# Low parts of transposed queries and keys, taken ahead of the evacuation copy of a step

## The chip, the core and the metric

One core of a Trainium2 chip runs the kernel. Its engines work side by side, each through its own queue of instructions in order: TensorE (PE; weight loads are PEld), VectorE (DVE), ScalarE (ACT), GpSimd (POOL), and SyncE (SP), which here only issues transfers. The metric is the device time of one execution in microseconds, less being better; the median of several executions is compared.

## What is computed

Attention in which the 12 heads are mixed twice, by `w_pre` ahead of the softmax and by `w_post` behind it, and then a two-layer network with a squared ReLU:

```python
# batch 4, heads 12, sequence 448, head size 64; d_ff 2048
scores = 1 / np.sqrt(64) * np.matmul(q, k.transpose(0, 1, 3, 2))
scores = np.einsum('bhij,hg->bgij', scores, w_pre)
scores = scores - np.max(scores, axis=-1, keepdims=True)
attn = np.exp(scores)
attn = attn / (np.sum(attn, axis=-1, keepdims=True) + 1e-09)
attn = np.einsum('bhij,hg->bgij', attn, w_post)
x = np.matmul(attn, v).transpose(0, 2, 1, 3).reshape(4 * 448, 12 * 64)
r = np.maximum(x @ w_in, 0.0)
out = (s * (r * r) + b) @ w_out
```

## The kernel before

Products that need full precision are made of three matmuls each: a number is split into a high part, which ScalarE writes as a rounded copy, and a low part, the difference, which VectorE takes. High times low, low times high and high times high are summed in one PSUM bank.

The attention part is cut into 16 chunks (4 per batch, 110 or 118 queries each), and a chunk into blocks of up to 10 queries, 180 blocks in all. A block has 120 rows: 10 queries by 12 heads. The loop at the end of the function runs one step `s` for each block, and several blocks are under way in each step: block `s + 5` is brought from the score tile `S` by a transfer (`relayout`, tile `blk`), block `s + 2` is split on GpSimd (`split`, tile `hl`), block `s` goes through `premix` (three matmuls into `pm`, L603; VectorE's maximum, L605; ScalarE's exponential with its sum, L610, and the sum's copy, L614), block `s - 1` is normalized (VectorE's reciprocal, L622; ScalarE's high part `eh`, L624; VectorE's `remainder`, L631), block `s - 3` goes through `postmix` (twelve matmuls into `po`, L646), and block `s - 4` is evacuated from PSUM to the tile `A` (`evacuate`, VectorE's copy at L662). There are two `po` banks, taken in turn.

Besides, a table (`plan`) says in which step the work of the chunks around falls. `prep_k` and `prep_q` transpose keys and queries on TensorE (`trk`, L457; `trq`, L479) into a PSUM tile with the tag `sc`; ScalarE writes the high part (`Tk`, L463; `Tq`, L483), and the low part is put on a list, `later`. A query tile is prepared in two halves, of four head pairs (here called full-sized) and of two (half-sized). `qk_pair` computes the scores of a head pair (six matmuls, `sc`, L504), in the same PSUM tile `sc`, which has one buffer, and ScalarE copies them to `S` (L514). So `sc` goes round: transpose, high and low part, score matmuls, copy to `S`, next transpose. `av_pair` (`xp`, L532, with ScalarE's copy `xs`, L554) multiplies with the values.

`low_parts` takes what stands on `later`, one VectorE subtraction each, all of them at L239. The loop calls it at the two places that the change's diff shows, and `prep_k`, `prep_q` and `qk_pair` call it at their start. The order on each engine is the order in which the code is written: no scheduler moves anything. VectorE also converts weights of the network, one operation per step where there is room (L157 to L181). Behind the loop come the two layers, at L254 and L311.

Of the kernel before, what the change touches and what calls it, by code (L numbers as in the profile page):

```python
# [21 lines left out]
def talking_heads_attention__then__act_relu2_kernel(  # L22
# [163 lines left out]
    def place_w(n):  # L186
        w_pool[n].tile([P, 2, 3 * P], F32R, tag=f"w{n}", name=f"place_{n}", bufs=1)

    def convert_step(upto):

        if done["run"] is None:
            if done["conv"] >= min(upto, len(units)):
                return False
            done["run"] = conversion(done["conv"])
        try:
            next(done["run"])
        except StopIteration:
            done["run"] = None
            done["conv"] += 1
        return True  # L200
# [13 lines left out]
    def load_x(r, b, kc):  # L214
        raw = rp.tile([P, S], F32, tag="xraw", name=f"xraw_{r}_{b}_{kc}", bufs=NKC)
        nc.sync.dma_start(raw, xd[b][kc])
        xraw_t[r, b, kc] = raw

    def split_x(r, b, kc):
        raw = xraw_t.pop((r, b, kc))  # L220
        if b == 1:

            if kc % 2 == 0:
                x_u["g"] = mp.tile(
                    [P, 2, PT], F32R, tag=f"g{kc // 2}_1", name=f"xg_{r}_{kc}", bufs=1
                )
            x = x_u["g"][:, :, kc % 2 * S:kc % 2 * S + S]
        else:
            x = rp.tile([P, 2, S], F32R, tag="x", name=f"x_{r}_{b}_{kc}", bufs=NKC)
        nc.scalar.activation(x[:, 0, :], raw, AF.Copy)  # L230
        later.append((x[:, 1, :], raw, x[:, 0, :]))
        x_u[r, b, kc] = x
# [3 lines left out]
    def low_parts():  # L236
        while later:
            o, x, hi = later.pop(0)
            nc.vector.tensor_tensor(out=o, in0=x, in1=hi.bitcast(F32), op=ALU.subtract)  # L239
# [323 lines left out]
    def qk_pair(ci, p):  # L563
        low_parts()
        for m in range(3):
            qk_part(ci, p, m)
# [9 lines left out]
    def relayout(t):  # L576
        ci, i0, ni = blocks[t]
        blk = blkp.tile([BP, S], F32, tag="blk", name=f"blk_{t}", bufs=LD)
        nb = first[ci + 1] - first[ci]
        r = t - first[ci]  # L580
        nc.sync.dma_start(blk[:ni * H, :], s_t[ci][r:r + nb * (ni - 1) + 1:nb, :, :])
        blk_t[t] = blk

    def split(t):
        n = blocks[t][2] * H
        blk = blk_t.pop(t)
        hl = blkp.tile([BP, 2, S], F32R, tag="hl", name=f"hl_{t}", bufs=2)
        nc.gpsimd.tensor_scalar(hl[:n, 0, :], blk[:n], 1.0, 0.0, op0=ALU.mult, op1=ALU.add)  # L588
        nc.gpsimd.tensor_tensor(  # L589
            out=hl[:n, 1, :], in0=blk[:n], in1=hl[:n, 0, :].bitcast(F32), op=ALU.subtract  # L590
        )
        hl_t[t] = hl

    def premix(t):
        n = blocks[t][2] * H
        hl = hl_t.pop(t)

        tag = "px" if t % 3 == 2 else "pm"
        pm = ps.tile([P, 512], F32, tag=tag, name=f"pm_{t}", bufs=banks.count(tag))
        for _ in range(2 if t < first[1] - 1 else 1 if t < first[1] + 3 else 0):  # L600
            nc.tensor.matmul(pm, keep[:, :P], keep, start=True, stop=True)
        for m, (w, x) in enumerate(((wpre_lo, 0), (wpre_hi, 1), (wpre_hi, 0))):
            nc.tensor.matmul(pm[:n, :S], w[:n, :n], hl[:n, x, :], start=(m == 0), stop=(m == 2))  # L603
        st = smp.tile([BP, 4], F32, tag="st", name=f"st_{t}")
        nc.vector.tensor_reduce(  # L605
            out=st[:n, 0:1], in_=pm[:n, :S], axis=AX.X, op=ALU.max, negate=True
        )

        e = pm[:, :S]
        nc.scalar.activation(e[:n], e[:n], AF.Exp, bias=st[:n, 0:1], accum_out=pm[:n, S:S + 1])  # L610
        e_t[t] = (e, st)

        total = pm[:, S:S + 1]
        nc.scalar.activation(  # L614
            st[:n, 2:3], total[:n], AF.Copy, scale=2.0 ** -15, bias=1e-9 * 2.0 ** -15
        )

    def normalize(t):

        n = blocks[t][2] * H  # L620
        e, st = e_t[t]
        nc.vector.reciprocal(st[:n, 3:4], st[:n, 2:3])  # L622
        eh = blkp.tile([BP, 2, S], F16, tag="eh", name=f"eh_{t}", bufs=3)
        nc.scalar.activation(eh[:n, 0, :], e[:n], AF.Copy, scale=st[:n, 3:4])  # L624
        eh_t[t] = eh

    def remainder(t):
        n = blocks[t][2] * H
        e, st = e_t.pop(t)
        eh = eh_t[t]  # L630
        nc.vector.scalar_tensor_tensor(  # L631
            out=eh[:n, 1, :], in0=e[:n], scalar=st[:n, 3:4], in1=eh[:n, 0, :],
            op0=ALU.mult, op1=ALU.subtract,
        )

    def postmix(t):
        ci, i0, ni = blocks[t]
        n = ni * H
        eh = eh_t.pop(t)
        if i0 == 0:  # L640
            a_t[ci] = ap_.tile([P, NC, H, CH], F32, tag="A", name=f"A_{ci}")
        po = ps.tile([P, 512], F32, tag="po", name=f"po_{t}", bufs=2)
        for c in range(NC):
            j0 = min(c * P, S - P)
            for m, (x, y) in enumerate(((1, 0), (0, 1), (0, 0))):
                nc.tensor.matmul(  # L646
                    po[:, c * BP:(c + 1) * BP],
                    eh[:n, x, j0:j0 + P],
                    wpost[:n, y].rearrange("p g i -> p (g i)"),
                    start=(m == 0),  # L650
                    stop=(m == 2),
                )
        po_t[t] = po

    def evacuate(t):
        ci, i0, ni = blocks[t]
        dst = a_t[ci][:, :, :, i0:i0 + ni]
        src = po_t.pop(t)[:, :NC * BP].rearrange("p (c g i) -> p c g i", c=NC, g=H)[:, :, :, :ni]
        if ci == NCH - 1:
            nc.scalar.activation(dst, src, AF.Copy)  # L660
        else:
            nc.vector.tensor_copy(dst, src)  # L662
# [6 lines left out]
    XA = 3  # L669
# [99 lines left out]
    def run_plan(step, early):  # L769

        k0 = state["next"]
        while k0 < len(plan) and plan[k0][0] < step + 1:
            _, order, _, f, args = plan[k0]
            if (order == 0) == early:
                f(*args)
            k0 += 1
        if not early:
            state["next"] = k0
            copy_x()
# [60 lines left out]
    tail = first[NCH - 1]  # L840
    for s in range(NB + 4):
        if s == tail - LD:
            early.close()
            rp = ctx.enter_context(tc.tile_pool(name="rp", bufs=1, side="right", reuse_waits="tile"))
            rp.tile([P, S], F32, tag="xraw", name="place_xraw", bufs=NKC)
            for n in range(NU_EARLY, NU_EARLY + NU_TAIL):
                w_pool[n] = rp
                place_w(n)
            rp.tile([P, X_GAP // 4], F32, tag="gap", name="gap_x", bufs=1)
            rp.tile([P, 2, S], F32R, tag="x", name="place_x", bufs=NKC)  # L850
            rp.tile([P, END_GAP // 4], F32, tag="end", name="gap_end", bufs=1)
        if s + LD < NB:
            relayout(s + LD)
        if s + LS < NB:
            split(s + LS)
        if 0 <= s - 1 < NB:
            ops = 7 * NU_EARLY
            if not later and turn["ops"] < ops * (s - CONV0) / (tail - LD - 2 * NP - CONV0):
                turn["ops"] += convert_step(NU_EARLY)
            normalize(s - 1)  # L860
        if 0 <= s - 4 < NB:
            evacuate(s - 4)
        if s <= tail - XA:
            low_parts()
        if s < NB:
            premix(s)
        low_parts()
        if s < 2:
            (build_scale, build_post)[s](*loaded_consts)
            qk_pair(1, NP - 2 + s)  # L870
        if 0 <= s - 1 < NB:
            remainder(s - 1)
        run_plan(s, True)
        if 0 <= s - 3 < NB:
            postmix(s - 3)
        run_plan(s, False)
        if 0 <= s - (tail - LD) < NKC // 2:
            for kc in range(2):
                load_x(0, 0, 2 * (s - (tail - LD)) + kc)
        if 0 <= s - (tail - XA) < NKC:  # L880
            split_x(0, 0, s - (tail - XA))
        if 0 <= s - tail < NKC:
            load_x(0, 1, s - tail)
# [111 lines left out]
```

## Time and profile before

| what | time |
|---|---|
| median of 3 runs | 938.13 us (937.76 to 938.72) |
| the profiled execution | 941.96 us |
| its span, from the first to the last instruction | 940.3 us |
| attention loop and what leads to it | to about 480 us of the span |
| the two layers | from there to the end |

The profile tells of one execution. Busy time of an engine is the sum of its instructions' times, in which an instruction that starts before its predecessor has quite ended counts in full. A wait is an engine's idle time ahead of an instruction, put down to what ended it. The chain that ended last is followed back from the last instruction, at each step to what released it or to its predecessor on its engine.

### The profile page before, as it was taken

The numbers are of one execution on the slowest core, as the hardware profiler recorded it, in microseconds if no ns is written. First come the engines' busy times: TensorE is split into PE (matmuls) and PEld (weight loads), VectorE is DVE, ScalarE is ACT, GpSimd is POOL, SyncE is SP. The second block draws the span as 40 slices with busy tenths as digits, with TensorE's granted clock in tenths as the row PEclk, the third lists the DMA queues.
The fourth block names the chain that finished last, engine by engine and source line by source line (L and its number), as shares of the span: only waits on it lengthen the run. The fifth ranks groups of instructions, "written<-read, shape, count | busy, mean of one in ns | idle before, by whom it ended". The sixth has DMA issues, their size and how long they took to land.

```text
span 940.3 us, 19909 instructions
## 1 busy us (share of the span) xinstructions
PE 917.5 (98%) x7538; PEld 786.3 (84%) x7538; DVE 655.2 (70%) x1364; ACT 567.3 (60%) x1264; POOL 396.5 (42%) x451
## 2 busy tenths in 40 slices
PE   8889999999999999999999999999999999999998
PEld 4567777777777777777789999999999999999998
DVE  3788888888888888888689139966405934976211
ACT  4687788887888888888877877221117687700000
POOL 3766677666767667767523324000002333300000
PEclk9999999999999999999999999999999999999999
DMA  4665645655466545646324213353510420255321
GB/s 99 168 166 134 165 113 148 160 149 156 123 157 158 144 122 144 164 134 184 101 73 143 76 59 85 89 172 126 177 43 26 143 93 17 75 161 185 127 93 51
DMA packets 126555, 115.22 MB, mean 123 GB/s; under 512 B 63960, under 2 KB 122348, under 8 KB 126460
## 3 DMA queue, kind: packets, MB, share of 16 engines
q1 hardware_dynamic: 116934, 102.28, 38.9%
q10 hardware_dynamic: 9366, 11.59, 3.4%
q8 instruction: 59, 0.97, 0.4%
q14 instruction: 36, 0.29, 0.1%
q0 software_dynamic: 160, 0.09, 0.1%
HBM read 58.87 MB, written 16.52 MB: 80 GB/s over the span
## 4 chain that ended last, share of the span: by engine, by line
PE 63%; ACT 17%; DVE 10%; DMA 7%; POOL 1%; issue 1%; SPq 1%; ACTq 0%; POOLq 0%; DVEq 0%
PE po L311 25%; PE ph L254 23%; ACT pm L610 6%; DMA blk<-S 5%; ACT S L514 4%; PE pm L603 4%; DVE A L662 3%; ACT eh L624 3%; PE sc L504 3%; PE xp L532 3%; PE po L646 3%; DVE st L605 2%; ACT st L614 2%; ACT xs L554 1%; PE ph_head L254 1%
## 5 line engine op out<-in xcount | busy, mean ns | idle before, releaser
L311 PE MATMUL po<-w,g 128*128 128x384 f32 x1344 | 233.5, 336 | 0.0
L311 PEld LDWEIGHTS po<-w,g 128*128 128x128 f32 x1344 | 233.0, 188 | 0.3 <-ACT ob L318 0.3
L589 POOL TENSOR_TENSOR hl<-blk,hl 120x448 fp32r<-120x448 f32 x180 | 205.9, 1144 | 15.0
L272 POOL TENSOR_TENSOR g<-h,g 128x448 fp32r<-128x448 f32 x64 | 79.4, 1240 | 280.1 <-ACT g L271 259.6
L254 PE MATMUL ph<-x,w 128*128 128x448 f32 x810 | 164.1, 362 | 0.0
L254 PEld LDWEIGHTS ph<-x,w 128*128 128x128 f32 x810 | 151.9, 188 | 10.2
L588 POOL TENSOR_SCALAR hl<-blk 120x448 fp32r<-120x448 f32 x180 | 104.6, 581 | 125.4 <-PE pm L603 102.9
L646 PEld LDWEIGHTS <-eh 120*128 120x128 f16 (+1 forms) x2160 | 115.3, 98 | 40.9 <-issue 40.5
L646 PE MATMUL po<-wpost,eh 120*128 120x120 f16 (+1 forms) x2160 | 144.7, 217 | 1.4 <-ACT A L660 1.4
L610 ACT ACTIVATE pm<-pm,st 120x448 f32<-120x448 f32 x180 | 110.1, 611 | 56.2 <-DVE st L605 55.7
L631 DVE SCALAR_TENSOR_TENSOR eh<-pm,st,eh 120x448 f16<-120x448 f32 x180 | 122.4, 680 | 26.2 <-ACT eh L624 22.9
L624 ACT ACTIVATE eh<-pm,st 120x448 f16<-120x448 f32 x180 | 114.6, 637 | 15.9 <-DVE st L622 15.6
L605 DVE TENSOR_REDUCE st<-pm 120x1 f32<-120x448 f32 x180 | 110.7, 615 | 7.4 <-PE pm L603 7.3
L662 DVE COPY A<-po 128x480 f32<-128x480 f32 x168 | 107.0, 637 | 0.1
L603 PE MATMUL pm<-hl,wpre_hi 120*120 120x448 f32 x360 | 101.9, 364 | 0.8 <-POOL hl L589 0.8
L532 PE MATMUL xp<-A,v 128*64 128x110 f32 (+1 forms) x1536 | 93.5, 265 | 0.0
L504 PE MATMUL sc<-Tk,Tq 64*110 64x448 f32 (+1 forms) x576 | 83.3, 395 | 8.4 <-DVE Tq L239 4.8
L514 ACT ACTIVATE S<-sc 110x896 f32<-110x896 f32 (+1 forms) x91 | 83.2, 914 | 10.0 <-PE sc L504 7.1
L603 PE MATMUL pm<-hl,wpre_lo 120*120 120x448 f32 x180 | 82.8, 460 | 0.1
L532 PEld LDWEIGHTS xp<-A,v 128*64 128x64 f32 x1536 | 74.2, 136 | 9.6 <-issue 0.9
L318 ACT ACTIVATE ob<-po 128x384 f32<-128x384 f32 x28 | 13.8, 493 | 98.0 <-PE po L311 86.0
L603 PEld LDWEIGHTS pm<-hl,wpre_hi 120*120 120x120 f32 x360 | 65.5, 182 | 5.6 <-POOL hl L589 1.0
(78 smaller groups left out, 981.9 us busy)
## 6 DMA issues: line engine op xcount, KB each, us to landing
blk<-S SPq DMA_DIRECT2D x172, 210.0 KB
raw<-in_moe_w_in_dram SPq DMA_DIRECT2D x32, 384.0 KB
raw<-in_moe_w_out_dram SPq DMA_DIRECT2D x32, 384.0 KB
xraw<-xd SPq DMA_DIRECT2D x48, 224.0 KB
part<-ob ACTq DMA_DIRECT2D x28, 192.0 KB
acc<-part SPq DMA_DIRECT2D x28, 192.0 KB
out_dram<-acc ACTq DMA_DIRECT2D x28, 192.0 KB
v<-in_v_dram SPq DMA_DIRECT2D x24, 192.0 KB
```

The source lines that it names most:

```text
L254: nc.tensor.matmul(ph[:, :S], w[:, i, c0:c0 + P], x[:, y, :], start=(kc == 0 and m == 0), stop=(kc == NKC - 1 and m == 2),)
L311: nc.tensor.matmul(po[:, :NO], g[:, x, c0:c0 + P], w[:, y, :], start=(f == 0 and m == 0), stop=(f == NF - 1 and m == 2),)
L514: nc.scalar.activation(s_t[ci][:n, 2 * p:2 * p + 2, :], x_t["two"][:n, :, :S], AF.Copy, scale=SCALE)
L532: nc.tensor.matmul(xp[e * D:(e + 1) * D, p % 4, :n], vt[:, e, c, :], a[:, c, 2 * p + e, :n], start=(c == 0), stop=(c == NC - 1),)
L589: nc.gpsimd.tensor_tensor(out=hl[:n, 1, :], in0=blk[:n], in1=hl[:n, 0, :].bitcast(F32), op=ALU.subtract)
L603: nc.tensor.matmul(pm[:n, :S], w[:n, :n], hl[:n, x, :], start=(m == 0), stop=(m == 2))
L605: nc.vector.tensor_reduce(out=st[:n, 0:1], in_=pm[:n, :S], axis=AX.X, op=ALU.max, negate=True)
L610: nc.scalar.activation(e[:n], e[:n], AF.Exp, bias=st[:n, 0:1], accum_out=pm[:n, S:S + 1])
L624: nc.scalar.activation(eh[:n, 0, :], e[:n], AF.Copy, scale=st[:n, 3:4])
L631: nc.vector.scalar_tensor_tensor(out=eh[:n, 1, :], in0=e[:n], scalar=st[:n, 3:4], in1=eh[:n, 0, :], op0=ALU.mult, op1=ALU.subtract,)
L646: nc.tensor.matmul(po[:, c * BP:(c + 1) * BP], eh[:n, x, j0:j0 + P], wpost[:n, y].rearrange("p g i -> p (g i)"), start=(m == 0), stop=(m = ...
L662: nc.vector.tensor_copy(dst, src)
```

## The change

Two calls in the loop change places. `low_parts()` was called behind `evacuate(s - 4)` and is now called ahead of it:

```diff
             normalize(s - 1)
+        if s <= tail - XA:
+            low_parts()
         if 0 <= s - 4 < NB:
             evacuate(s - 4)
-        if s <= tail - XA:
-            low_parts()
         if s < NB:
             premix(s)
```

`tail - XA` is three steps ahead of the last chunk's first block. The instructions of TensorE, ScalarE, GpSimd and SyncE keep their order; VectorE's differs at 46 places, 18 with a low part of keys (`Tk`) and 28 with one of queries (`Tq`), 14 of these full-sized and 14 half-sized. All 46 look alike.

VectorE at the step in which the sixth key pair of the second batch gets its low part (`Tk_5`; the last number of a name is the build's), before and after; the lines with - and + show where the subtraction stood and stands:

```order
 L631 SCALAR_TENSOR_TENSOR eh_1911<-pm_1864,st_1868,eh_1911 120x448
 L622 RECIPROCAL st_1918<-st_1918 120x1
+L239 TENSOR_TENSOR Tk_5_1942<-trk_5_1937,Tk_5_1942 128x448
 L662 COPY A_1923<-po_1924 128x48x10
-L239 TENSOR_TENSOR Tk_5_1942<-trk_5_1937,Tk_5_1942 128x448
 L605 TENSOR_REDUCE st_1958<-pm_1954 120x1
 L631 SCALAR_TENSOR_TENSOR eh_1950<-pm_1914,st_1918,eh_1950 120x448
```

The subtraction now stands directly behind the reciprocal, and the evacuation copy between it and the maximum of the step.

ScalarE at the same step, the same before and after; `Tk_5` at L463 is the high part that this subtraction reads:

```order
L610 ACTIVATE pm_1914<-pm_1914,st_1918 120x448
L614 ACTIVATE st_1918<-pm_1914 120x1
L463 ACTIVATE Tk_5_1942<-trk_5_1937 128x448
L624 ACTIVATE eh_1950<-pm_1914,st_1918 120x448
L610 ACTIVATE pm_1954<-pm_1954,st_1958 120x448
L614 ACTIVATE st_1958<-pm_1954 120x1
L514 ACTIVATE S_1617<-sc_4_1986 110x896
```

Nothing moved here: the high part follows the sum's copy (L614) that the reciprocal of this step reads, and the next exponential (L610) reads the maximum.

VectorE at a step with a half-sized low part of queries (`Tq`, two head pairs of 110 queries):

```order
 L622 RECIPROCAL st_2258<-st_2258 108x1
+L239 TENSOR_TENSOR Tq_2026<-trq_1_2276,Tq_2026 128x2x110
 L662 COPY A_1923<-po_2263 128x48x10
-L239 TENSOR_TENSOR Tq_2026<-trq_1_2276,Tq_2026 128x2x110
 L605 TENSOR_REDUCE st_2294<-pm_2290 120x1
```

The same two instructions have changed places.

## Rows read from the trace of the kernel before

**Rows 1.** The page, part 1: busy us (share of the span) and instructions.

```profile
PE 917.5 (98%) x7538; PEld 786.3 (84%) x7538; DVE 655.2 (70%) x1364; ACT 567.3 (60%) x1264; POOL 396.5 (42%) x451
```

**Rows 2.** Busy time in one stretch: us, engines (instructions), granted clock, transfers.

```profile
60.00:435.00 375.00, 366.23 (x4189) 276.97 (x4189) 325.34 (x698) 305.75 (x770) 258.79 (x303) 1.00 0.54 143
```

**Rows 3.** Waits from 60 to 435 us: us in total, times, longest.

```profile
ACT pm L610 <- DVE st L605: 48.5, 72, 1.1
...
PE sc L504 <- DVE Tq L239: 4.1, 14, 0.4
...
PE trq L479 <- ACT S L514: 2.1, 5, 1.1
...
PE sc L504 <- DVE Tk L239: 1.2, 3, 0.7
```

**Rows 4.** The chain that ended last, 222 to 234 us: start, us, what.

```profile
222.44 0.53 DVE Tk L239
222.97 0.54 DVE st L605
...
223.54 0.68 ACT pm L610 x2
...
224.41 0.81 ACT S L514
...
232.51 0.54 DVE Tk L239
...
233.09 0.86 PE sc L504 x6
```

**Rows 5.** Timeline at a full-sized low part: start, us, engine, line, operation [idle before].

```profile
119.18 0.54 ACT L463 ACTIVATE Tk<-trk 128x448 fp32r<-128x448 f32 x1
...
119.40 0.64 DVE L662 COPY A<-po 128x480 f32<-128x480 f32 x1
...
119.95 0.61 DVE L239 TENSOR_TENSOR Tk<-trk,Tk 128x448 fp32r<-128x448 f32 x1
120.48 0.61 DVE L605 TENSOR_REDUCE st<-pm 120x1 f32<-120x448 f32 x1
...
120.62 0.86 PE L504 MATMUL sc<-Tk,Tq 64*110 64x448 f32 x6
...
121.13 0.61 ACT L610 ACTIVATE pm<-pm,st 120x448 f32<-120x448 f32 x1 [0.89 <-DVE st L605]
...
122.12 0.81 PE L646 MATMUL po<-wpost,eh 120*128 120x120 f16 x12
```

**Rows 6.** Timeline of the prologue: a high part and the low part that waits for it.

```profile
16.47 0.55 ACT L463 ACTIVATE Tk<-trk 128x448 fp32r<-128x448 f32 x1 [0.46 <-PE trk L457]
...
17.05 0.62 DVE L239 TENSOR_TENSOR Tk<-trk,Tk 128x448 fp32r<-128x448 f32 x1 [0.53 <-ACT Tk L463]
```

**Rows 7.** Timeline at a half-sized low part.

```profile
138.63 0.35 ACT L483 ACTIVATE Tq<-trq 128x220 fp32r<-128x220 f32 x1
...
138.85 0.64 DVE L662 COPY A<-po 128x480 f32<-128x480 f32 x1
...
139.40 0.38 DVE L239 TENSOR_TENSOR Tq<-trq,Tq 128x220 fp32r<-128x220 f32 x1
...
139.84 0.87 PE L504 MATMUL sc<-Tk,Tq 64*110 64x448 f32 x6 [0.28 <-DVE Tq L239]
```

**Rows 8.** Timeline: copies to S and the transposes behind them, first and last place.

```profile
77.80 0.91 ACT L514 ACTIVATE S<-sc 118x896 f32<-118x896 f32 x1
...
78.83 0.37 PE L479 MATMUL trq<-ident,nq 118*128 118x118 f32 x2
...
346.07 0.91 ACT L514 ACTIVATE S<-sc 110x896 f32<-110x896 f32 x1
...
347.04 0.60 PE L479 MATMUL trq<-ident,nq 110*128 110x110 f32 x4
```

**Rows 9.** Timeline of ScalarE: a copy to S that waits for a transfer.

```profile
101.22 0.92 ACT L514 ACTIVATE S<-sc 110x896 f32<-110x896 f32 x1 [0.41 <-DMA nk<-in_k_dram]
```

## The prediction

> **What bounds the kernel now.** I read the busy times first, then the stretch of the attention loop alone, then who waited for whom there, then the chain that ended last, and at the end single places of the timeline. Over the span TensorE is busy 98% of the time and VectorE 70% [rows 1]. The change reaches only the attention loop, where 46 low parts (18 of keys, 28 of queries) change places with an evacuation copy. In 375 us of that loop TensorE is busy 366.23 us at a granted clock of 1.00, VectorE 325.34 and ScalarE 305.75 [rows 2]. So TensorE seems to be the bound, with 8.8 us of shown idle time. The waits say where some of that is: TensorE's score matmuls `sc` wait for the low part 4.1 us (queries) and 1.2 us (keys), and transposes of queries wait 2.1 us for ScalarE's copy of a score tile, `S` [rows 3]. But the longest wait is ScalarE's: the exponential at L610 waits 48.5 us, 72 times, for VectorE's maximum at L605 [rows 3].
>
> Whether that wait costs anything, the chain tells. It runs through low part (L239), maximum (L605), exponential (L610), and the copy of scores (L514) on ScalarE [rows 4]; ahead of the low part stand, in the same chain, the sum's copy, the reciprocal and the evacuation copy. This is a ring of in-order queues: ScalarE can't go on to the next exponential before the maximum is there, and the maximum stands on VectorE behind copy and low part. Of the 46 low parts the chain passes 24 in this way; 13 times it goes from the low part to the score matmuls instead, as at 232.51 [rows 4]; 9 it doesn't touch. So in the loop two bounds lie side by side: TensorE with almost no gaps, and a VectorE-ScalarE ring that is as long.
>
> **The change part by part.** No instruction is added or taken away, and only VectorE's queue is in another order. At each of 46 places the row recip, copy, low part, maximum becomes recip, low part, copy, maximum.
>
> *The new wait, full-sized low parts (32 of the 46).* The low part needs the rounded high part that ScalarE writes just before. At the place shown that copy runs from 119.18 for 0.54, to 119.72, while VectorE starts the evacuation at 119.40 and the low part at 119.95 [rows 5]. Today the evacuation covers the whole of ScalarE's copy. Moved ahead, the low part finds VectorE free at 119.40 and its input not there. In the prologue, where VectorE does wait for the same operation, it starts at 17.05 behind a copy that runs from 16.47 for 0.55, thus 0.03 us behind its end [rows 6]. So the low part would start at 119.75: 0.20 us earlier than now, with VectorE idle for 0.35 us. The evacuation follows 0.53 us later (119.95 to 120.48 is what a low part holds the queue [rows 5]), at 120.28 instead of 119.40, and the maximum 0.55 us behind that, at 120.83 instead of 120.48: **0.35 us later**. Queued behind the waiting low part are the evacuation, the maximum and the remainder; ScalarE's exponential waits for the maximum (0.89 us of idle time ended by it at 121.13 [rows 5]) and so goes 0.35 us later too.
>
> *Half-sized low parts of queries (14).* ScalarE's copy is shorter: 138.63 for 0.35, with the evacuation at 138.85 and the low part at 139.40 [rows 7]. By the same working the low part starts at 139.01, 0.39 us earlier, VectorE idles 0.16 us, and the maximum comes **0.16 us later**. There TensorE's score matmul waited 0.28 us for the low part [rows 7]; that wait goes.
>
> *The evacuation itself* ends 0.88 us later, at about 120.92. I cost it at nothing: the next postmix into the same PSUM bank is the one of the next step, at 122.12 [rows 5], 1.2 us behind. If that cover were gone, TensorE would wait directly. The output tile that it fills is read from the step after the last evacuation of a chunk.
>
> *What of it lies on the path.* Delayed exponentials delay `S`, and the next transpose needs the bank that `S` reads. In three stretches, 76 to 123, 189 to 236 and 300 to 347 us, the transposes start 0.05 to 0.14 us behind the end of `S`; there are 21 such low parts that no other wait covers, the first with `S` at 77.80 for 0.91 and the transpose at 78.83, the last with `S` at 346.07 for 0.91 and the transpose at 347.04 [rows 8]. Fifteen are full and six half: 15 x 0.35 + 6 x 0.16 = 6.2 us. In each stretch one low part leads on the chain to score matmuls whose `S` no transpose waits for; there I take the whole gain, 3 x 0.20 = 0.6 us. In each stretch one more is covered, as `S` waits for a transfer or a matmul anyway (0.41 us at 101.22 [rows 9]): 0. That leaves 5.6 us. Of the other 19 low parts the chain passes seven to the maximum (six half, one full: 6 x 0.16 + 0.35 = 1.3 us lost) and seven to the score matmuls (at 0.20 us, 1.4 us won); five it doesn't touch. Net -0.1. Sum: **5.5 us longer**.
>
> *Its bounds.* If none of the transposes follows and only the old chain counts, 12 full and 12 half delays less 13 gains of 0.20 give 4.2 + 1.9 - 2.6 = 3.5 us. If the gains at the score matmuls aren't taken, because TensorE is still at work or the delayed `S` is what is late next, 6.2 + 1.3 = 7.5 us. I take the middle, since both branches leave from the same low part and the later one counts.
>
> A rule speaks for the change. The waits show TensorE's shown gaps at the score matmuls, 4.1 and 1.2 us [rows 3], on the engine with the most busy time [rows 2]. The Trainium skill (Perfetto Trace Analysis, Optimization Strategy) says to find the gaps of the most-contended engine, see what its instructions wait for, and make those dependencies start sooner. By that rule the low part is the right thing to bring forward and the kernel gets faster (the first rival below); by the chain in rows 4 the gap is moved to the next transpose and grows.
>
> **The rivals.** *Faster, TensorE alone is the bound.* The waits at the score matmuls go and the delayed exponentials are hidden. For it: 98% busy, and 5.3 us of waits for low parts in the loop [rows 3]. The half-sized ones gain 0.39 us against waits of 0.28, so these go whole; the full ones gain 0.20 against waits of up to 0.7 us, so some stay. Worth some 4.5 us: 938.1 - 4.5 = 933.6 us. It decides if transposes have slack behind `S` of more than 0.35 us; at the 21 places they have 0.05 to 0.14 [rows 8].
>
> *No change.* The 0.35 us are taken up at the transfers and matmul stretches between the ring's stretches, or the gains at the score matmuls, counted on TensorE's side, equal the losses. For it: three such covers are seen, and TensorE shows few gaps. Against it: the ring's links are queue order and data, with nothing between them that gives way. Time 938 to 940 us.
>
> *All is paid.* If every low part counts with its whole wait, 32 x 0.35 + 14 x 0.16 = 13.4 us: 951.5 us. Against it: nine low parts stand off the chain, and three in the stretches named are covered by another wait.
>
> *It doesn't do what it says.* Should ScalarE's copies have ended by the time VectorE comes free, there is no wait, and the low parts come 0.55 us earlier at no cost; but the two rows [rows 5, 7] show the copy still running, and nothing in the change moves it.
>
> **How the numbers follow.** The profiled execution took 941.96 us, its span 940.3; the median of the runs shown is 938.13. The difference of 3.8 us (0.4%) lies outside what the change touches, so I put the 5.5 us on the median: 943.6 us. Chances: forecast 0.69 (its own range 941.6 to 945.6, by the bounds), all paid or most of it 0.08, no change 0.14, faster 0.09. What a measurement here can tell from no change is about 0.2%, 1.9 us; faster than that 0.09, within it 0.14, slower 0.77. The range from 938.3 to 949.0 leaves out the faster case, about half of no change, and the upper part of all paid.
>
> **What would show it.** In the profile after: VectorE's low parts show a wait for ScalarE's L463 or L483 in the loop, 0.35 us full and 0.16 half, some 13 us in sum. The wait of L610 for L605 grows by about that sum. TensorE's waits of `sc` for low parts nearly go, and those of transposes for `S` grow by several microseconds, in the three stretches above all. The linear layers after 480 us keep their length. I am wrong if the low parts show no wait, or if the waits of L610 grow and the three stretches keep their lengths.

## The result, and the profile after

The changed kernel takes 947.64 us (median of 4 runs, 947.34 to 949.78) against 938.35 us: 1.0101 times as long, with an interval from 1.0088 to 1.0113. That is 9.3 us more, where 5.5 were forecast; the direction was right and the size came out short.

The busy times are those of [rows 1] to within 3.2 us per engine. What has changed is who waits. Waits of the kernel after, 60 to 440 us (us in total, times, longest), beside [rows 3]:

```profile
ACT pm L610 <- DVE st L605: 61.6, 70, 1.3
...
PE trq L479 <- ACT S L514: 8.0, 17, 0.8
...
DVE Tk L239 <- ACT Tk L463: 4.9, 18, 0.3
PE trk L457 <- ACT S L514: 4.8, 12, 0.7
DVE Tq L239 <- ACT Tq L483: 3.6, 13, 0.3
...
PE sc L504 <- DVE Tk L239: 0.5, 1, 0.5
```

VectorE's new wait is there, at 18 low parts of keys and 13 of queries. The exponential waits 13 us longer for the maximum. TensorE's wait of the score matmuls for low parts of queries is gone and that for keys nearly so, and in its place TensorE waits 12.8 us for `S` ahead of transposes. Before, these were 2.1 us for transposes of queries [rows 3] and 0.2 us for those of keys, in the same view from 60 to 435 us:

```profile
PE trk L457 <- ACT S L514: 0.2, 1, 0.2
```

The gap has moved, and has grown.

One full-sized place, the one of [rows 5] (timeline of the kernel after: start, us, engine, line, operation [idle before]):

```profile
118.21 0.54 ACT L463 ACTIVATE Tk<-trk 128x448 fp32r<-128x448 f32 x1
118.35 0.16 DVE L622 RECIPROCAL st<-st 120x1 f32<-120x1 f32 x1
...
118.78 0.62 DVE L239 TENSOR_TENSOR Tk<-trk,Tk 128x448 fp32r<-128x448 f32 x1 [0.27 <-ACT Tk L463]
119.33 0.65 DVE L662 COPY A<-po 128x480 f32<-128x480 f32 x1
...
119.51 0.87 PE L504 MATMUL sc<-Tk,Tq 64*110 64x448 f32 x6
119.89 0.61 DVE L605 TENSOR_REDUCE st<-pm 120x1 f32<-120x448 f32 x1
...
120.54 0.61 ACT L610 ACTIVATE pm<-pm,st 120x448 f32<-120x448 f32 x1 [1.27 <-DVE st L605]
...
121.31 0.91 ACT L514 ACTIVATE S<-sc 110x896 f32<-110x896 f32 x1
...
122.27 0.41 PE L479 MATMUL trq<-ident,nq 110*128 110x110 f32 x2 [0.45 <-ACT S L514]
```

The low part starts 0.03 us behind the end of ScalarE's copy (118.75). The exponential's wait has grown from 0.89 to 1.27 us. The score matmuls start at once, but end at 120.38, while `S` starts only at 121.31, behind exponential and sum; and the transpose, 0.05 us behind `S` as before, is now waited for by TensorE. At a half-sized place, beside [rows 7]:

```profile
138.54 0.35 ACT L483 ACTIVATE Tq<-trq 128x220 fp32r<-128x220 f32 x1
...
138.68 0.16 DVE L622 RECIPROCAL st<-st 108x1 f32<-108x1 f32 x1
...
138.92 0.39 DVE L239 TENSOR_TENSOR Tq<-trq,Tq 128x220 fp32r<-128x220 f32 x1
139.22 0.65 DVE L662 COPY A<-po 128x480 f32<-128x480 f32 x1
139.40 0.87 PE L504 MATMUL sc<-Tk,Tq 64*110 64x448 f32 x6
139.79 0.61 DVE L605 TENSOR_REDUCE st<-pm 120x1 f32<-120x448 f32 x1
...
140.44 0.61 ACT L610 ACTIVATE pm<-pm,st 120x448 f32<-120x448 f32 x1 [0.93 <-DVE st L605]
```

Two rows of before at the same place:

```profile
138.77 0.17 DVE L622 RECIPROCAL st<-st 108x1 f32<-108x1 f32 x1
...
140.35 0.61 ACT L610 ACTIVATE pm<-pm,st 120x448 f32<-120x448 f32 x1 [0.75 <-DVE st L605]
```

No idle time stands at this low part, yet it starts 0.24 us behind the reciprocal's start, where in before the copy, which shows no wait, came 0.08 us behind it (138.85 [rows 7]). The reciprocal's own row hides the short wait; the exponential's 0.93 us instead of 0.75 shows it.

The chain of the kernel after, 216 to 220 us, beside [rows 4] (start, us, what):

```profile
216.32 0.57 ACT pm L610 x2
...
216.91 0.17 ACT st L614
217.08 0.44 ACT Tk L463
...
217.54 0.62 DVE Tk L239
218.17 0.56 DVE A L662
218.73 0.54 DVE st L605
...
219.30 0.68 ACT pm L610 x2
```

ScalarE's high part is a link of the ring now. The chain passes 36 of the 46 low parts by this link, and 34 of them go on to the copy and the maximum; before, 24 went on to the maximum.

The profiled spans must not be subtracted: 945.6 less 940.3 is 5.3 us, but the profiled execution of before had a late prologue, and was itself 3.8 us above its median. A better mark is the reciprocal that stands ahead of each of the 46 low parts, in the same place of VectorE's order before and after. The first of them starts at 36.81 us in the profile of before and at 33.81 in that of after, ahead of all that the change touches. From the first to the last it is 379.44 us before (36.81 to 416.25) and 387.99 after (33.81 to 421.80): 8.55 us more, close to the medians' 9.3. What comes behind the last mark takes the same time, 524.05 and 523.80 us. By stretch, from reciprocal to reciprocal:

| stretch, by before | before | after | more |
|---|---|---|---|
| 36.81 to 75.45 | 38.64 | 38.61 | 0.0 |
| 75.45 to 124.23 | 48.78 | 51.22 | 2.4 |
| 124.23 to 188.43 | 64.20 | 64.30 | 0.1 |
| 188.43 to 236.73 | 48.30 | 51.01 | 2.7 |
| 236.73 to 299.97 | 63.24 | 63.72 | 0.5 |
| 299.97 to 348.40 | 48.43 | 50.87 | 2.4 |
| 348.40 to 416.25 | 67.85 | 68.26 | 0.4 |

The same marks give each single place: the time from its reciprocal to that of the next place, after less before, is what the place adds. Three reciprocals on end, in before and in after:

```profile
90.38 0.17 DVE L622 RECIPROCAL st<-st 120x1 f32<-120x1 f32 x1
...
98.12 0.17 DVE L622 RECIPROCAL st<-st 120x1 f32<-120x1 f32 x1 [0.19 <-ACT st L614]
...
103.46 0.16 DVE L622 RECIPROCAL st<-st 120x1 f32<-120x1 f32 x1
```
```profile
88.11 0.16 DVE L622 RECIPROCAL st<-st 120x1 f32<-120x1 f32 x1
...
95.67 0.16 DVE L622 RECIPROCAL st<-st 120x1 f32<-120x1 f32 x1 [0.20 <-ACT st L614]
...
101.38 0.16 DVE L622 RECIPROCAL st<-st 120x1 f32<-120x1 f32 x1
```

From the first to the second it is 7.74 us before and 7.56 after: this place wins 0.18 us. From the second to the third it is 5.34 and 5.71: that place loses 0.37. Most places are like one of these. Added up in the groups of the prediction, taken from the chain of before:

| group in the prediction | places | forecast | measured |
|---|---|---|---|
| three stretches, maximum later | 21 | 6.2 | 6.75 |
| three stretches, gain at the score matmuls | 3 | -0.6 | -0.28 |
| three stretches, covered by another wait | 3 | 0 | 1.12 |
| elsewhere, chain to the maximum | 7 | 1.3 | 0.46 |
| elsewhere, chain to the score matmuls | 6 of 7 (the last has no mark behind it) | -1.2 | -1.10 |
| elsewhere, not touched by the chain | 5 | 0 | 1.60 |
| sum | 45 | 5.7 | 8.55 |

These are single executions. How far they can be trusted, three runs below tell, in which only some places are changed: an unchanged place adds or takes 0.03 us at most there, except at two of them, whose low parts stand at 53.46 and 176.21 us in before. The latter takes 0.55 us less than in before in runs that leave it alone too; that stands in the 0.46 of the fourth row, which would be 1.0 without it.

### The profile page after: what moved, and what is told of

Same layout as the page of the kernel before. It is cut to its first block, busy times and chain, and to the rows that moved or that the text cites. A ratio compares the mean times of both kernels' runs of the same rounds, so it can differ in the third digit from the quotient of the medians.

```text
span 945.6 us, 19909 instructions
## 1 busy us (share of the span) xinstructions
PE 916.2 (97%) x7538; PEld 785.4 (83%) x7538; DVE 658.4 (70%) x1364; ACT 566.3 (60%) x1264; POOL 397.3 (42%) x451
## 4 chain that ended last, share of the span: by engine, by line
PE 63%; ACT 21%; DVE 10%; DMA 5%; issue 1%; POOL 0%; ACTq 0%; SPq 0%; POOLq 0%
PE po L311 25%; PE ph L254 23%; ACT pm L610 7%; ACT S L514 6%; PE pm L603 4%; ACT eh L624 3%; PE xp L532 3%; DVE st L605 3%; DVE A L662 3%; PE po L646 3%; DMA blk<-S 3%; PE sc L504 2%; ACT st L614 2%; DVE Tq L239 1%; PE ph_head L254 1%; ACT xs L554 1%
## 5 line engine op out<-in xcount | busy, mean ns | idle before, releaser
L610 ACT ACTIVATE pm<-pm,st 120x448 f32<-120x448 f32 x180 | 110.0, 611 | 70.1 <-DVE st L605 69.8
```

## The experiments

The theory: VectorE now waits for ScalarE's high part, everything behind the low part comes later, and it is the delayed maximum that costs. The rivals: the late evacuation costs; or TensorE alone is the bound and the waits at the score matmuls decide.

**One kind of low part at a time.** The order of before, with the low parts of one kind moved:

```diff
             normalize(s - 1)
+        if s <= tail - XA and later and len(later[0][0].shape) == 2:
+            low_parts()
         if 0 <= s - 4 < NB:
```

This is for keys; for queries the condition asks for the four or the two head pairs instead.

> Only the 18 low parts of keys stand ahead of the evacuation copy; the 28 of queries stay behind it. Theory (VectorE waits for ScalarE's high part, and the maximum and the exponential behind it come later by about 0.37 us at a full-sized place): 18 x 0.37 = 6.7 us at most, a place or two covered, so 5 to 6.5 us slower than before. Rival, TensorE alone is the bound: no change or up to 1.5 us faster, as TensorE's waits for low parts of keys go.

Measured: 1.0051 (1.0033 to 1.0070), 4.8 us (3.1 to 6.6). The middle lies a little under the theory's span, the interval reaches into it, and the rival is out. By the marks the 18 places add 5.3 us in this run, the same as in the kernel after.

> Only the 14 full-sized low parts of queries stand ahead of the evacuation copy. Theory: the maximum comes 0.37 us later at each, 5.2 us if all were paid; some are taken back later in the chunk, so 1.5 to 4 us slower than before. By the prediction's working these places cost nothing net (delays and gains of seven each cancel): within 1 us of before.

Measured: 1.0019 (1.0003 to 1.0035), 1.8 us (0.3 to 3.3). Slower, but the interval reaches from the one expectation into the other. The marks of its trace say more: the 14 places add 1.1 us together, or 1.65 without the 0.55 us that the place at 176.21 us takes less in runs that leave it alone too. (By the prediction's own groups these places are four delays, six gains and four at nothing, 0.2 us net, and not seven and seven.) The six gains came, 0.16 to 0.23 us each. What did not come out is the nothing: the four places that the chain doesn't touch add 0.36 to 0.52 us each.

> Only the 14 half-sized low parts of queries stand ahead of the evacuation copy. Theory: the maximum comes 0.19 us later at each, 2.7 us if all were paid: 0.5 to 2.7 us slower than before. Rival, TensorE's waits of about 0.28 us at the score matmuls count, and these go here: up to 3 us faster than before.

Measured: 1.0015 (1.0005 to 1.0025), 1.4 us (0.5 to 2.3). TensorE's waits of the score matmuls for low parts of queries fell here from 4.1 us [rows 3] to 1.3, and the kernel is slower all the same. The three ratios add up to 0.85% against the change's 1.01%, within their intervals: more than half is the keys'.

**The maximum late, and low part and copy in place.** The order of before, with one instruction on VectorE that does no useful work:

```diff
         if s <= tail - XA:
+            n = 0 if not later else 1 if later[0][0].shape[1] == 2 else 2
             low_parts()
+            if n:
+                nc.vector.tensor_reduce(
+                    out=mx[:, 0:n], in_=ident.unsqueeze(1).to_broadcast([P, n, P]),
+                    axis=AX.X, op=ALU.max,
+                )
```

> The order is that of before, with one more instruction on VectorE at each of the 46 places, between low part and maximum (a maximum over a constant tile whose result is read by nothing; two rows' worth at full-sized places, one at half-sized ones, about 0.33 and 0.2 us of the queue). The low part and the evacuation of the step stand where they stood; only the maximum comes later. Theory (delay of the maximum alone): as slow as the change, 7 to 11 us slower than before. Rival (what costs is the evacuation that comes 0.5 to 0.9 us later, or something else in the low part's new place): within 2 us of before.

Measured: 1.0119 (1.0101 to 1.0137), 11.2 us. Its timeline at the same place:

```profile
120.20 0.64 DVE L662 COPY A<-po 128x480 f32<-128x480 f32 x1
...
120.76 0.61 DVE L239 TENSOR_TENSOR Tk<-trk,Tk 128x448 fp32r<-128x448 f32 x1
121.29 0.41 DVE L867 TENSOR_REDUCE mx<-ident 128x2 f32<-128x256 f32 x1
...
121.62 0.61 DVE L605 TENSOR_REDUCE st<-pm 120x1 f32<-120x448 f32 x1
...
122.27 0.61 ACT L610 ACTIVATE pm<-pm,st 120x448 f32<-120x448 f32 x1 [1.22 <-DVE st L605]
```

Copy and low part stand 0.56 us apart (0.55 in before), and the pad puts 0.33 us between low part and maximum. That alone costs as much as the change, within the intervals. By the marks it does so at the same places: in the three stretches each of the 15 full-sized places that the prediction counted adds 0.32 us here and 0.37 in the change, which is in both what the maximum is late by, though only in the change the copy is late too. So the late evacuation isn't needed for the loss, and adds nothing that shows. At the nine places of the second and fifth row, where the change gains, the pad adds nothing, less than 0.1 us in all: there the late maximum doesn't count, and what the change wins is the low part that comes earlier. Five half-sized places outside the stretches add 0.5 us each with the pad, against 0.14 to 0.32 in the change; why, isn't shown. (With the maximum the remainder behind it comes later too, in both kernels; the postmix reads its result two steps later.)

**Three other orders.** First, the maximum ahead of both:

```diff
-        if 0 <= s - 4 < NB:
+        last = s - 4 >= first[NCH - 1]
+        if 0 <= s - 4 < NB and last:
             evacuate(s - 4)
-        if s <= tail - XA:
-            low_parts()
         if s < NB:
             premix(s)
         low_parts()
+        if 0 <= s - 4 < NB and not last:
+            evacuate(s - 4)
```

> VectorE's order in every step is reciprocal, maximum, low part, evacuation copy (the last chunk's evacuation stays where it was, on ScalarE). The low part stands where it stood before in time (behind one operation of 0.55 us), so it has no wait for ScalarE; the maximum comes up to 1.1 us earlier at the 46 places and 0.55 us earlier in the other steps; the evacuation comes 1.1 us later at the 46 places, later than in the change. Theory (the place of the maximum decides): faster than before, by 3 to 9 us, as far as TensorE's gaps of 8.8 us in the loop allow. Rival (the late evacuation is what costs): slower than before by more than the change's 9 us.

Measured: 0.9949 (0.9930 to 0.9968), 4.8 us faster than before, with the evacuation later than in the change. A copy this late doesn't cost 9 us. But the copy stands behind the maximum in every step here, so the gain is not that of the 46 places alone. The waits of this kernel, 60 to 435 us, show what is late next:

```profile
ACT S L514 <- PE sc L504: 40.1, 69, 0.9
PEld L646 <- DVE A L662: 9.9, 28, 0.4
```

ScalarE no longer waits for the maximum; now `S` waits for the score matmuls. A late evacuation does hold the postmix's weight loads here, 9.9 us; its matmuls wait for it only 0.8 us over the whole span.

Second, the low part ahead as in the change, and the copy behind the maximum (the code of the kernel just shown, with the first `low_parts()` kept ahead of `premix` and `evacuate` right behind `premix`):

> VectorE's order is reciprocal, low part, maximum, evacuation copy: the low part ahead as in the change, with its wait for ScalarE, but the copy no longer between it and the maximum. Theory: the wait stays (0.27 us and less), the maximum comes 0.2 us earlier than before at full-sized places, and 0.55 us earlier in the steps without a low part, so faster than before by 2 to 8 us, the score matmuls' waits gone as well. Rival (late evacuation): about as slow as the change or slower.

Measured: 0.9914 (0.9892 to 0.9936), 8.1 us faster than before (930.74 us median): the fastest of all. Its timeline at the same place, and its busy times from 60 to 435 us beside [rows 2]:

```profile
116.46 0.62 DVE L239 TENSOR_TENSOR Tk<-trk,Tk 128x448 fp32r<-128x448 f32 x1 [0.27 <-ACT Tk L463]
...
117.00 0.61 DVE L605 TENSOR_REDUCE st<-pm 120x1 f32<-120x448 f32 x1
117.40 0.85 PE L504 MATMUL sc<-Tk,Tq 64*110 64x448 f32 x6
117.53 0.65 DVE L662 COPY A<-po 128x480 f32<-128x480 f32 x1
117.65 0.61 ACT L610 ACTIVATE pm<-pm,st 120x448 f32<-120x448 f32 x1 [0.70 <-DVE st L605]
```
```profile
60.00:435.00 375.00, 374.46 (x4296) 283.96 (x4295) 329.57 (x717) 311.32 (x788) 266.26 (x312) 1.00 0.56 151
```

VectorE waits for the high part exactly as in the change, 0.27 us, and still the kernel is faster than before; only the copy no longer stands between that wait and the maximum. TensorE is busy 374.46 of 375 us, with 107 more matmuls done in the same stretch (4296 against 4189). Its median is also 3.5 us below that of the order just shown, from which it differs in the low part's place alone (the two intervals just touch): ahead of the maximum, with its wait, the low part seems better placed than behind it. So what the wait costs depends on what is queued behind it. How much of the 8.1 us comes from the 46 places and how much from the other steps, these two runs don't tell.

Third, the low part behind the maximum (the first `low_parts()` left out):

> VectorE's order is reciprocal, evacuation copy, maximum, low part: at the 46 places the maximum comes about 0.53 us earlier and the low part 0.55 us later than before; nothing else changes. It prices the other branch, the low part's way to the score matmuls. Theory: TensorE's waits at the score matmuls grow by up to 46 x 0.55 = 25 us, part of which the earlier exponentials don't give back: 3 to 15 us slower than before. Rival (the low part's place matters little and the maximum alone decides): up to 9 us faster than before.

Measured: 1.0189 (1.0164 to 1.0215), 17.7 us slower than before, beyond what was expected. The waits, 60 to 435 us:

```profile
ACT S L514 <- PE sc L504: 32.4, 51, 0.9
...
ACT pm L610 <- DVE st L605: 26.4, 68, 0.6
PE sc L504 <- DVE Tq L239: 17.3, 26, 1.0
PE sc L504 <- DVE Tk L239: 7.8, 18, 1.1
```

The maximum is earlier and the exponential's wait for it nearly halved (48.5 us before [rows 3]), but the score matmuls now wait 25.1 us for the low parts, which stand 0.55 us later. So the branch from the low part to the score matmuls has no half microsecond to spare: later by that much, it is the bound.

## Why the prediction was right in direction and short in size

- **The new wait.** Worked out from the prologue's 0.03 us and the two copies, it came as said: the low part at a full-sized place starts 0.43 us behind the reciprocal's start, 0.08 us behind it is where a successor that waits for nothing starts, so it waits 0.35 us. Of that the profile shows 0.27 as idle. The maximum came 0.37 us later rather than 0.35 (the exponential's wait went from 0.89 to 1.27), and 0.19 rather than 0.16 at half-sized places (0.75 to 0.93). Over the 21 places of the first term that is 15 x 0.02 + 6 x 0.03 = 0.5 us more, and 0.5 us more is what the table has.
- **The evacuation at nothing.** Right: with the pad the copy isn't late, and the places lose as much.
- **The step that failed is the places priced at nothing.** Three full-sized low parts were called covered, as `S` waits there for something else anyway, and five were left out because the old chain doesn't touch them. Together they were to add 0 and added 2.7 us, nearly all of what was missing: seven of the eight lost 0.36 to 0.52 us each, as much as the maximum's delay or more (the eighth is the one at 53.46 us, which is uneven in runs that leave it alone as well). The cover named is the wait of 0.41 us at 101.22 [rows 9]. In the kernel after it is still there:

```profile
99.14 0.92 ACT L514 ACTIVATE S<-sc 110x896 f32<-110x896 f32 x1 [0.40 <-DMA nk<-in_k_dram]
```

  `S` starts 3.47 us behind the reciprocal of this place (95.67), where it was 3.10 (98.12): the wait has moved along by 0.37 us and has covered nothing. What it is that holds `S` there, and moves along, isn't shown. The five others rest on a reading of the chain that goes too far: it follows one path, and a place that it passes by may be just as tight on another.
- **The gains at the score matmuls came.** Ten low parts were credited with 0.20 us each; of the nine with a mark behind them eight gained 0.15 to 0.24 us, and the one at 204.00 lost 0.08. That is -1.4 us where -1.8 were forecast. "The later one counts" held place by place: at the places credited the earlier low part counted, at nearly all others the later maximum. So it is luck that the upper bound named, 7.5 us, which leaves the gains out, lies near the 8.55 measured: it drops a term that was there, and lacks one that was bigger.
- **The rivals.** That TensorE alone is the bound fell: its waits at the score matmuls did go, and it waits more elsewhere. By the Trainium skill (Perfetto Trace Analysis, Optimization Strategy) the gaps of the most-contended engine are what to close; the trace agrees that they closed, from 5.3 to 0.5 us, and disagrees that this helps here, by 9.3 us, as VectorE and ScalarE beside it were held up by more. In the fastest order TensorE's waits for low parts and for `S` add up to 0.5 us from 60 to 435 us, and there the time fell. That all is paid came nearer to the truth than the chance of 0.08 says: 34 of the 45 places with a mark behind them lose 0.14 us or more. It overstates because of the gains.
- **What would show it.** The wait of L610 grew by 13 us as said. VectorE's shown wait is 8.5 us and not 13, since the idle column starts only where the predecessor's row ends. What stands behind the last mark, with the two layers in it, kept its length, as said.

## What to carry to other kernels

Moving work ahead on an in-order engine pays only if its input is there by then; look up when the producer ends, not only when the consumer begins, and ask what is queued behind. Where a chain forks, ask at each place which branch is the later one, and price that branch. Don't price a place at nothing because the chain that ended last passes it by, or because another wait seems to cover it: a wait that hangs on the same ring moves along. And if something must stand between a wait and the critical result, move the thing whose delay costs least: here the evacuation copy, behind the maximum, which beats both kernels.

## What the runs showed of the hardware that I had not expected

A short wait on VectorE can be invisible. Behind a reciprocal of 0.16 us the half-sized low part started 0.24 us after the reciprocal's start, where a successor that waited for nothing started 0.08 us after it, and the trace showed no idle time and named no releaser; only the wait of the next engine grew, by 0.18 us.
